# Top-k attention and a hardswish feed-forward on one core: another order of the first loads, warm-up matmuls, and another place for a weight conversion's low words

## The chip, the cores and the metric

The kernel runs on one core of one Trainium2 chip. The metric is the device time of one execution in microseconds, and the kernel before takes 1570.19 us (median of 3 runs, 1567.33 to 1574.13). The engines are called by the profile's names: PE (TensorE, matmuls; PEld its weight loads), DVE (VectorE), ACT (ScalarE), POOL (GpSimd) and SP (SyncE, which here only issues DMAs).

## What is computed

```python
def _attn_ref(q, k, v):                       # each (8, 8, 576, 64)
    scores = scale * np.matmul(q, k.transpose(0, 1, 3, 2))
    kth = np.partition(scores, -32, axis=-1)[..., -32:-31]
    scores = np.where(scores >= kth, scores, -1000000000.0)
    attn = np.exp(scores - np.max(scores, axis=-1, keepdims=True))
    attn = attn / (np.sum(attn, axis=-1, keepdims=True) + 1e-09)
    return np.matmul(attn, v).astype(np.float32)

x = attn_out.transpose(0, 2, 1, 3).reshape(4608, 512)
h = x @ w_in                                  # (512, 2048)
g = h * np.clip(h + 3.0, 0.0, 6.0) / 6.0
out = (g @ w_out).astype(np.float32)          # (2048, 512)
```

Every row of scores keeps its 32 largest values; the attention's output goes through a feed-forward with a hardswish gate. q, k and v come as float32, w_in and w_out as float64, that is as two 32-bit words for each number. The kernel makes float32 of them itself.

## The kernel before

**Tiles.** Two heads make a pair, four pairs make a batch. `Pair.load` (L146) brings k and q of a pair into one tile `landed`: for each of k and q two DMAs of 128 KB and one of 32 KB with the 64 rows that are left beyond 512. `Pair.transpose` (L171) turns them with nine matmuls against `ident` (L177) into a PSUM tile `big`, the only one of its tag (five banks), and ACT copies it to `kq` (kT and qT) and `kr` (the left part of k). A `Duo` is two pairs and one block of 128 queries (or the 64 left ones). `Duo.scores` (L201) forms the score products: a left part for both heads (L232) and 512 columns for each head (L238), then copies them from PSUM to `sc` (L239, L242).

**Top 32.** For each pair of a duo (u = 0, 1) `top` (L249) makes four rounds of MAX8 (L256), two rows each, and, between them, MATCH_REPLACE8 (L260). That is DVE's main work. The rest of the attention follows in slots: `shift` (POOL), `exp` (ACT, L279 and L284), `inverse` (DVE, L293), `weights` (POOL, L303 and a copy to 16-bit halves, L312), `flip` (a DMA transpose, L318), `join` (a copy by ACT or POOL, L324), `values` (PE, L344) and `place` (ACT, L354). The feed-forward (`feed_forward`, L358) is cut into pieces that are put between: h (L371), gate (ACT L379, L381; POOL L385, L386), acc (L391), o (L401). h, acc and pv take PSUM tiles of tag w, of which there are three. The gate's g and, in the conversion, a and y take tiles of tag g, of which there are eight.

**Order.** The order of the instructions on each engine is the program's order (`manual_schedule`). The loop at L572 goes over the duos `m` and eight slots `i` each; in every slot stands a round of `top`, then what the table `usual` or `early` (for the first two duos) has put there, a conversion step, and some pieces of the feed-forward. An engine works its queue in that order and stops at the first instruction that has to wait.

**Conversion of the weights.** There are 32 chunks of 128x512 numbers, 16 of w_in and then 16 of w_out. `convert` (L96) is a generator in stages: a DMA brings the 512 KB of a chunk into `st` (L102); ACT takes the high words' magnitude into `a` (L108), POOL clamps it (L109), and ACT turns the low words into a small fraction `y` (L111); later DVE shifts `a` (L117) and gives `y` the sign (L118); later POOL adds both as integers into the weights (L123). `convert_step` (L495) makes one stage of up to three chunks and asks for another load: chunk n's DVE part stands two steps after its ACT part, its POOL add one step after that. Three steps stand before the loop, and one in each slot.

**The start** (L517 to L529): load pair 0, load two chunks, load pair 1, transpose pair 0, a step, scores of pair 0, a step, load pair 2, a step, transpose pair 1, scores of pair 1, another chunk. Pair 3 is loaded in slot 0. All DMAs are issued by SP. In the before-order of DVE one conversion stands ahead of the first MAX8.

Of the kernel before, what the change touches and what calls it, by code (L numbers as in the profile page):

```python
# [29 lines left out]
def kernel(  # L30
# [32 lines left out]
    gpool = pool("g", 8)  # L63
# [3 lines left out]
    ps_w = pool("ps_w", 3, space=PSUM)  # L67
# [5 lines left out]
    ident = const([P, P], "ident")  # L73
# [4 lines left out]
    w_out = const([P, NFC, DM], "w_out")  # L78
# [9 lines left out]
    def big():  # L88

        return ps_big.tile([P, 5 * 512], F32, tag="big", name="big")  # L90
# [2 lines left out]

    WC = 512

    def convert(dst, src):  # L96

        st = kqpool.tile([P, 2 * WC], U32, tag="kq", name="st")
        nc.sync.dma_start(st[:], src)  # L102
        yield
        words = st[:].rearrange("p (n two) -> p n two", two=2)
        lo, hi = words[:, :, 0], words[:, :, 1]
        a = gpool.tile([P, WC], F32, tag="g", name="a")
        y = gpool.tile([P, WC], F32, tag="g", name="y")
        nc.scalar.activation(a[:], hi.bitcast(F32), AF.Abs)  # L108
        nc.gpsimd.tensor_scalar(a[:], a[:], HI_MOST, HI_LEAST, ALU.min, ALU.max)  # L109

        nc.scalar.activation(y[:], lo, AF.Copy, bias=2.0, scale=2.0**-51)  # L111
        yield

        au, yu = a[:].bitcast(U32), y[:].bitcast(U32)
        nc.vector.tensor_scalar(au, au, 3, None, ALU.logical_shift_left)  # L117
        nc.vector.scalar_tensor_tensor(  # L118
            out=yu, in0=hi, scalar=0x80000000, in1=yu,
            op0=ALU.bitwise_and, op1=ALU.bitwise_or,  # L120
        )
        yield
        nc.gpsimd.tensor_tensor(  # L123
            dst.bitcast(I32), a[:].bitcast(I32), y[:].bitcast(I32), ALU.add
        )

    def weight_chunks():
# [11 lines left out]
    class Pair:  # L139
# [3 lines left out]
            self.b, self.hp = b, hp  # L143
            self.vm, self.vr, self.kr = vms[hp], vrs[hp], krs[b % 2 * NHP + hp]

        def load(self):  # L146
            h0 = 2 * self.hp
            t = self.landed = kqpool.tile([P, 2 * J + 1, 2, D], F32, tag="kq", name="landed")
            for i, src in enumerate((k, q)):
                for hh in range(2):  # L150
                    nc.sync.dma_start(
                        t[:, i * J : (i + 1) * J, hh, :],
                        src[self.b, h0 + hh, 0:JP, :].rearrange("(p j) d -> p j d", j=J),
                    )
                nc.sync.dma_start(
                    t[i * R : (i + 1) * R, 2 * J, :, :],
                    src[self.b, h0 : h0 + 2, JP:S, :].rearrange("h s d -> s h d"),
                )
# [9 lines left out]
                    self.vr[hh * R : (hh + 1) * R, hh, :], v[self.b, h0 + hh, JP:S, :]  # L168
                )

        def transpose(self):  # L171
            kq = kqpool.tile([P, JP + S], F32, tag="kq", name="kq")
            self.kT, self.qT = kq[:, 0:JP], kq[:, JP : JP + S]
            ps = big()
            for j in range(2 * J + 1):
                rows = self.landed[:, j, :, :].rearrange("p h d -> p (h d)")
                nc.tensor.transpose(ps[:, j * P : (j + 1) * P], rows, ident[:])  # L177
            c0 = 2 * JP
            nc.scalar.copy(kq[:, 0:c0], ps[:, 0:c0])
            nc.scalar.copy(kq[:, c0 : c0 + R], ps[:, c0 + R : c0 + 2 * R])  # L180
            for hh in range(2):
                d = slice(hh * D, (hh + 1) * D)
                nc.scalar.copy(self.kr[d, hh, :], ps[d, c0 : c0 + R])

    class Duo:

# [14 lines left out]
        def scores(self, us=(0, 1)):  # L201

            if us[0] == 0:
                self.sc = scpool.tile([P, 2, 2 * (S + R)], F32, tag="sc", name="sc")
                self.den = mpool.tile([P, 2, 2], F32, tag="den", name="den")
            sc, nu = self.sc[:, us[0] : us[-1] + 1, :], len(us)
            ps = big()
            heads = [slice(0, D), slice(D, P)]
            qs = slice(self.qt * P, min(self.qt * P + P, S))
            banks = ps[:, 0 : 4 * 512].rearrange("p (n s) -> p n s", s=512)  # L210
            left = ps[:, 4 * 512 :]
            if self.rest:


                quarters = [
                    (i, hh, d, heads[u ^ hh])
                    for i, u in enumerate(us)
                    for hh, d in enumerate(heads)
                ]
                for i, hh, d, to in quarters:  # L220
                    pr = self.pairs[us[i]]
                    nc.tensor.matmul(banks[to, i, :], pr.qT[d, qs], pr.kT[d, :])
                for i, hh, d, to in quarters:
                    pr = self.pairs[us[i]]
                    nc.tensor.matmul(banks[to, 2 + i, 0:R], pr.qT[d, qs], pr.kr[d, hh, :])
                nc.gpsimd.memset(sc[:, :, S : S + R], 0.0)
                nc.scalar.copy(sc[:, :, 0:JP], banks[:, 0:nu, :])
                nc.scalar.copy(sc[:, :, JP:S], banks[:, 2 : 2 + nu, 0:R])
                return
            for i, u in enumerate(us):  # L230
                pr = self.pairs[u]
                nc.tensor.matmul(  # L232
                    left[:, i * P : (i + 1) * P], pr.qT[:, qs], pr.kr[:].rearrange("p h r -> p (h r)")
                )
            for i, u in enumerate(us):
                pr = self.pairs[u]
                for hh, d in enumerate(heads):
                    nc.tensor.matmul(banks[:, 2 * i + hh, :], pr.qT[d, qs], pr.kT[d, :])  # L238
            nc.scalar.copy(  # L239
                sc.rearrange("p u (h s) -> p (u h) s", h=2)[:, :, 0:JP], banks[:, 0 : 2 * nu, :]  # L240
            )
            nc.scalar.copy(  # L242
                sc[:, :, JP : JP + P], left[:, 0 : nu * P].rearrange("p (u r) -> p u r", r=P)
            )

        def row(self, u, t):
            return self.sc[:, u, t * S : (t + 1) * S]
# [162 lines left out]
    duos = []  # L410
# [77 lines left out]
    def land(count=1):  # L488

        for _ in range(min(count, len(chunks))):  # L490
            c = convert(*chunks.pop(0))
            next(c)
            landing.append(c)

    def convert_step():  # L495


        for c in adding:
            next(c, None)
# [15 lines left out]
        return pairs[b + 1][at - first] if b + 1 < B and 0 <= at - first < NHP else None  # L515

    first = pairs[0]  # L517
    first[0].load()
    land(2)
    first[1].load()  # L520
    first[0].transpose()
    convert_step()
    duos[0].scores((0,))
    convert_step()
    first[2].load()
    convert_step()
    first[1].transpose()
    duos[0].scores((1,))
    land()  # L529

# [41 lines left out]
    for m in range(ND + 3):  # L572
        u = duos[m] if m < ND else None
        for i in range(8):
            if u:
                u.top(i // 4, i % 4)
            if m < 4:
                parts(8 * m + i, False)
            convert_step()
            if m == 0 and i == 0:  # L580
                first[3].load()
            if m == 0 and i in (1, 2):
                first[i + 1].transpose()
            if i == (4 if m == 0 else 1) and m + 1 < ND:
                duos[m + 1].scores()
            if m < 4:
                parts(8 * m + i, True)
            else:
                parts(8 * m + i)
            if m == 0 and i in (1, 4):  # L590
                for p in duos[i // 4].pairs:
                    p.load_values()
            if i == 0:
                p = pair_at(m, 4)
                if p:
# [48 lines left out]
```

## Time and profile before

| what | value |
|---|---|
| span of the profiled execution | 1567.3 us |
| DVE busy | 1466.7 us, 94% |
| PE busy | 1446.8 us, 92% |
| POOL busy | 1143.8 us, 73% |
| ACT busy | 1097.0 us, 70% |
| MAX8 (L256) | 0.74 us each, 1152 of them |
| MATCH_REPLACE8 (L260) | 0.74 us each, 864 of them |
| L117, 32 times | 0.40 / 0.53 / 1.79 us (min / median / max) |
| L118, 32 times | 0.68 / 0.68 / 1.75 us |
| POOL's add L123, 32 times | 1.26 / 1.27 / 1.72 us |
| first MAX8 starts | 13.58 us |
| DVE's last conversion starts | 142.1 us |

The profile is one execution, in microseconds from the span's start. A row of its timeline gives start, length, engine, line, operation and tiles; in square brackets stand the time that the engine sat idle before it and what ended that. An instruction that stands on an engine but waits for a memory port counts as busy there, so a row that is longer than the shortest of its kind can hide a wait. In the chain of work that ended last, "issue" is time for which the profile shows no wait.

### The profile page before, as it was taken

How to read it: one execution, taken by the hardware profiler on the slowest of the kernel's cores; microseconds unless marked ns; L12 is line 12 of the kernel's file. 1: busy time of each engine (PE TensorE's matmuls, PEld its weight loads, DVE VectorE, ACT ScalarE, POOL GpSimd, SP SyncE). 2: the span in 40 equal slices, each digit the busy share in tenths (PEclk: the TensorE clock that was granted, in tenths of full speed). 3: DMA queues.
4: the chain of work that ended last, by engine and by line, in shares of the span. 5: the costliest groups of instructions: out<-in, count | busy, mean ns of one | idle time of the engine just before them, and what ended most of it. 6: DMA issues, size and time to landing. Idle time of an engine off the chain costs nothing.

```text
span 1567.3 us, 28748 instructions
## 1 busy us (share of the span) xinstructions
PE 1446.8 (92%) x10272; PEld 1033.0 (66%) x10272; DVE 1466.7 (94%) x3105; ACT 1097.0 (70%) x1865; POOL 1143.8 (73%) x1264
## 2 busy tenths in 40 slices
PE   5356898899999999999999999999999999999899
PEld 3142665577776777667777777667767777666675
DVE  6999999999999998999999999999999999999910
ACT  6675776777777777777767777777777777777631
POOL 4868688677777788677777779677777778777761
PEclk9977799999999999999999999999999999999999
DMA  8551545444344545345344454344343544433420
GB/s 238 155 188 39 117 87 101 85 92 83 69 83 98 98 83 104 70 100 100 71 85 83 102 99 86 86 99 98 68 83 83 98 99 90 97 68 68 79 43 14
DMA packets 450319, 144.49 MB, mean 92 GB/s; under 512 B 433280, under 2 KB 441472, under 8 KB 450176
## 3 DMA queue, kind: packets, MB, share of 16 engines
q1 hardware_dynamic: 450176, 142.65, 44.2%
q8 instruction: 81, 1.33, 0.3%
q14 instruction: 62, 0.51, 0.1%
HBM read 45.09 MB, written 9.44 MB: 35 GB/s over the span
## 4 chain that ended last, share of the span: by engine, by line
DVE 42%; PE 40%; POOL 6%; ACT 5%; issue 4%; DMA 1%; SPq 1%; POOLq 0%; ACTq 0%
DVE m L256 22%; DVE wk L260 18%; PE h L371 15%; PE acc L391 15%; PE pv L344 5%; PE big L238 3%; POOL e L312 2%; DVE y L118 1%; POOL sc L303 1%; DMA t<-e 1%; ACT eT L324 1%; ACT sc L284 1%; PE big L177 1%; DVE a L117 1%; POOL eT L324 1%
## 5 line engine op out<-in xcount | busy, mean ns | idle before, releaser
L256 DVE MAX8 m<-wk 128x8 f32<-128x576 f32 x864 | 612.6, 745 | 2.2
L391 PE MATMUL acc<-w_out,g 128*128 128x512 f32 x1152 | 522.7, 604 | 17.3 <-POOL g L386 17.3
L371 PEld LDWEIGHTS h<-xT,w_in 128*128 128x128 f32 x4096 | 469.6, 193 | 37.3 <-issue 19.5
L371 PE MATMUL h<-xT,w_in 128*128 128x128 f32 x4096 | 482.7, 277 | 12.0 <-ACT xT L354 12.0
L260 DVE MATCH_REPLACE8 wk<-m,wk 128x576 f32<-128x576 f32 x576 | 423.3, 741 | 0.0
L391 PEld LDWEIGHTS acc<-w_out,g 128*128 128x128 f32 x1152 | 214.4, 193 | 263.5 <-issue 235.8
L303 POOL TENSOR_SCALAR sc<-sc,den 128x576 f32<-128x576 f32 x288 | 213.2, 750 | 206.1 <-DVE den L293 184.6
L312 POOL COPY e<-sc 128x2304 uint16<-128x2304 uint16 (+1 forms) x192 | 320.0, 1677 | 10.1
L324 ACT COPY eT<-t 128x2304 uint16<-128x2304 uint16 (+1 forms) x82 | 216.0, 2635 | 48.1 <-DMA t<-e 47.7
L279 ACT ACTIVATE sc<-sc,m 128x576 f32<-128x576 f32 x288 | 210.6, 779 | 52.3 <-DVE m L256 51.9
L284 ACT ACTIVATE sc<-sc,shift 128x576 f32<-128x576 f32 x288 | 220.4, 770 | 35.3 <-POOL shift L272 33.0
L344 PE MATMUL pv<-eT,vm 128*64 128x128 f32 (+1 forms) x2560 | 163.7, 272 | 56.0 <-ACT eT L324 44.2
L260 DVE MATCH_REPLACE8 wk<-m,sc 128x576 f32<-128x576 f32 x288 | 211.6, 741 | 0.0
L324 POOL COPY eT<-t 128x2304 uint16<-128x2304 uint16 (+1 forms) x78 | 203.5, 2609 | 6.0 <-DMA t<-e 5.8
L344 PEld LDWEIGHTS pv<-eT,vm 128*64 128x64 f32 x2560 | 135.0, 141 | 108.0 <-ACT eT L324 48.9
L256 DVE MAX8 m<-sc 128x8 f32<-128x576 f32 x288 | 203.0, 741 | 1.4 <-ACT sc L242 1.4
L379 ACT ACTIVATE g<-h,three 128x512 f32<-128x512 f32 x144 | 98.9, 687 | 146.7 <-PE h L371 136.0
L386 POOL TENSOR_TENSOR g<-g,hs 128x512 f32<-128x512 f32 x144 | 185.0, 1284 | 12.2 <-POOL g L385 0.2
L239 ACT COPY sc<-big 128x2048 f32<-128x2048 f32 (+1 forms) x65 | 118.9, 1829 | 34.0 <-PE big L238 33.8
L385 POOL TENSOR_SCALAR g<-g 128x512 f32<-128x512 f32 x144 | 88.9, 618 | 68.5 <-ACT g L379 58.9
L238 PE MATMUL big<-kq 64*128 64x512 f32 x512 | 135.5, 649 | 0.0
L381 ACT COPY hs<-h 128x512 f32<-128x512 f32 x144 | 83.8, 582 | 0.0
(47 smaller groups left out, 1030.6 us busy)
## 6 DMA issues: line engine op xcount, KB each, us to landing
landed<-in_k_dram SPq DMA_DIRECT2D x64, 128.0 KB, 2.8
landed<-in_q_dram SPq DMA_DIRECT2D x64, 128.0 KB, 2.9
st<-in_moe_w_in_dram SPq DMA_DIRECT2D x16, 512.0 KB, 5.0
vm<-in_v_dram SPq DMA_DIRECT2D x64, 128.0 KB, 2.3
st<-in_moe_w_out_dram SPq DMA_DIRECT2D x16, 512.0 KB, 6.2
out_dram<-o SPq DMA_DIRECT2D x32, 256.0 KB, 2.5
t<-e SPq DMA_TRANSPOSE x160, 4.6
landed<-in_k_dram SPq DMA_DIRECT2D x32, 32.0 KB, 2.5
```

The source lines that it names most:

```text
L238: nc.tensor.matmul(banks[:, 2 * i + hh, :], pr.qT[d, qs], pr.kT[d, :])
L256: nc.vector.max(self.m[u][:, t, 8 * r : 8 * r + 8], self.cur[t])
L260: nc.vector.match_replace(wk, self.m[u][:, t, 8 * r : 8 * r + 8], self.cur[t], LOWEST)
L279: nc.scalar.activation(row, row, AF.Prelu, bias=m[:, t, TOP_K - 1 : TOP_K], scale=-1.0, alpha=FLAT)
L284: nc.scalar.activation(row, row, AF.Exp, bias=self.less[u][:, t : t + 1], scale=-scale / FLAT, accum_out=self.den[:, u, t : t + 1],)
L303: nc.gpsimd.tensor_scalar(row, row, self.den[:, u, t : t + 1], 1.0, ALU.mult, ALU.mult)
L312: nc.gpsimd.tensor_copy(halves[:, :, to : to + c1 - c0], words)
L324: copy(eT[:, 0 : self.nb, :] .rearrange("p c q -> p (c q)") .bitcast(U16) .rearrange("p (x h) -> p h x", h=2), self.t16[u][:, 0 : 2 * self ...
L344: nc.tensor.matmul(pv[hh * D : (hh + 1) * D, u * w : (u + 1) * w], pr.vm[:, hh, c, :] if c < J else pr.vr[:, hh, :], rhs, start=(c == 0), ...
L371: nc.tensor.matmul(h[:, (f - f0) * P : (f - f0 + 1) * P], w_in[:, i, f * P : (f + 1) * P], xT[:, i, :], start=(i == 0), stop=(i == NHP - 1),)
L386: nc.gpsimd.tensor_tensor(g[:], g[:], hs[:], ALU.mult)
L391: nc.tensor.matmul(acc[:], gs[f // nf][:, f % nf * P : (f % nf + 1) * P], w_out[:, f, :], start=(f == 0), stop=(f == NFC - 1),)
```

## The change

There are four edits. The first batch is loaded first: q of pair 0 is issued by ACT instead of SP, the three other pairs are loaded ahead of most weight chunks, and the loads of chunks follow one by one; one conversion step before the loop is gone. For pair 0 the transposes go to three PSUM tiles of tag w, each copied as soon as it is ready, and the part of q that the first scores do not need is copied later; of the first scores the left part is copied first and then each head by itself. A warmed-up TensorE: DVE clears one block of w_out, and PE multiplies it twice into a PSUM tile that nothing reads, while the first loads are under way. The low words y no longer take a tile of tag g: for the first 16 chunks (those of w_in) ACT writes them to a PSUM tile of tag w and DVE writes the signed word to the weights' place; for the 16 chunks of w_out ACT writes them to the weights' place at once. POOL's add then reads a and the destination.

```diff
-    def convert(dst, src):
+    def convert(dst, src, early):
...
-        y = gpool.tile([P, WC], F32, tag="g", name="y")
+        y = ps_w.tile([P, WC], F32, tag="w", name="y")[:] if early else dst
...
-        nc.scalar.activation(y[:], lo, AF.Copy, bias=2.0, scale=2.0**-51)
+        nc.scalar.activation(y, lo, AF.Copy, bias=2.0, scale=2.0**-51)
...
-            out=yu, in0=hi, scalar=0x80000000, in1=yu,
+            out=dst.bitcast(U32), in0=hi, scalar=0x80000000, in1=y.bitcast(U32),
...
-            dst.bitcast(I32), a[:].bitcast(I32), y[:].bitcast(I32), ALU.add
+            dst.bitcast(I32), a[:].bitcast(I32), dst.bitcast(I32), ALU.add
...
-        def load(self):
+        def load(self, queue=None):
...
-            for i, src in enumerate((k, q)):
+            for i, (src, eng) in enumerate(((k, nc.sync), (q, queue or nc.sync))):
                 for hh in range(2):
-                    nc.sync.dma_start(
+                    eng.dma_start(
...
+            if first:
+                ps = [ps_w.tile([P, 512], F32, tag="w", name="kqp") for _ in range(3)]
+                turn(ps[0], range(J))
+                turn(ps[1], [J, 2 * J])
+                turn(ps[2], range(J + 1, 2 * J))
+                nc.scalar.copy(self.kT, ps[0][:])
+                nc.scalar.copy(kq[:, JP : JP + P], ps[1][:, 0:P])
+                copy_left(ps[1][:, P:])
+                self.later = [
+                    (kq[:, JP + P : c0], ps[2][:, 0 : JP - P]),
+                    (kq[:, c0 : c0 + R], ps[1][:, P + R : 2 * P]),
+                ]
+                return
...
+            if us == (0,):
+                (to, src), rest = copies
+                copies = [rest, (to[:, 0, :], src[:, 0, :]), (to[:, 1, :], src[:, 1, :])]
+            for copy in copies:
+                nc.scalar.copy(*copy)
...
-            c = convert(*chunks.pop(0))
+            c = convert(*chunks.pop(0), early=len(chunks) >= NFC)
...
-    first[0].load()
-    land(2)
+    nc.vector.memset(w_out[:, 0, :], 0.0)
+    ps = big()
+    for _ in range(2):
+        nc.tensor.matmul(ps[:, 0:DM], w_out[:, 0, 0:P], w_out[:, 0, :])
+    first[0].load(nc.scalar)
     first[1].load()
-    first[0].transpose()
+    land()
+    first[2].load()
+    land()
+    first[0].transpose(first=True)
+    duos[0].scores((0,))
+    for copy in first[0].later:
+        nc.scalar.copy(*copy)
     convert_step()
-    duos[0].scores((0,))
+    first[3].load()
+    first[1].transpose()
     convert_step()
-    first[2].load()
-    convert_step()
-    first[1].transpose()
     duos[0].scores((1,))
     land()
...
-            if m == 0 and i == 0:
-                first[3].load()
```

More of the change, by code (lines that the diff above doesn't have):

```diff
@@ L106, in convert @@
         a = gpool.tile([P, WC], F32, tag="g", name="a")
-        y = gpool.tile([P, WC], F32, tag="g", name="y")
+        y = ps_w.tile([P, WC], F32, tag="w", name="y")[:] if early else dst
         nc.scalar.activation(a[:], hi.bitcast(F32), AF.Abs)
         nc.gpsimd.tensor_scalar(a[:], a[:], HI_MOST, HI_LEAST, ALU.min, ALU.max)
-        nc.scalar.activation(y[:], lo, AF.Copy, bias=2.0, scale=2.0**-51)
+        nc.scalar.activation(y, lo, AF.Copy, bias=2.0, scale=2.0**-51)
         yield
-        au, yu = a[:].bitcast(U32), y[:].bitcast(U32)
+        au = a[:].bitcast(U32)
         nc.vector.tensor_scalar(au, au, 3, None, ALU.logical_shift_left)
         nc.vector.scalar_tensor_tensor(
-            out=yu, in0=hi, scalar=0x80000000, in1=yu,
+            out=dst.bitcast(U32), in0=hi, scalar=0x80000000, in1=y.bitcast(U32),
             op0=ALU.bitwise_and, op1=ALU.bitwise_or,
@@ L154, in load @@
                     )
-                nc.sync.dma_start(
+                eng.dma_start(
                     t[i * R : (i + 1) * R, 2 * J, :, :],
@@ L169, in load_values, with transpose, turn, copy_left @@
                 )
-        def transpose(self):
+        def transpose(self, first=False):
             kq = kqpool.tile([P, JP + S], F32, tag="kq", name="kq")
             self.kT, self.qT = kq[:, 0:JP], kq[:, JP : JP + S]
+            c0 = 2 * JP
+            def turn(ps, tiles):
+                for i, j in enumerate(tiles):
+                    rows = self.landed[:, j, :, :].rearrange("p h d -> p (h d)")
+                    nc.tensor.transpose(ps[:, i * P : (i + 1) * P], rows, ident[:])
+            def copy_left(ps):
+                for hh in range(2):
+                    d = slice(hh * D, (hh + 1) * D)
+                    nc.scalar.copy(self.kr[d, hh, :], ps[d, 0:R])
+            if first:
[11 more added lines that the diff above has]
+                return
             ps = big()
[L175 to L178, printed above, removed]
+            turn(ps, range(2 * J + 1))
             nc.scalar.copy(kq[:, 0:c0], ps[:, 0:c0])
             nc.scalar.copy(kq[:, c0 : c0 + R], ps[:, c0 + R : c0 + 2 * R])
-            for hh in range(2):
-                d = slice(hh * D, (hh + 1) * D)
-                nc.scalar.copy(self.kr[d, hh, :], ps[d, c0 : c0 + R])
+            copy_left(ps[:, c0:])
     class Duo:
@@ L238, in scores @@
                     nc.tensor.matmul(banks[:, 2 * i + hh, :], pr.qT[d, qs], pr.kT[d, :])
[L239 to L244, printed above, removed]
+            copies = [
+                (sc.rearrange("p u (h s) -> p (u h) s", h=2)[:, :, 0:JP], banks[:, 0 : 2 * nu, :]),
+                (sc[:, :, JP : JP + P], left[:, 0 : nu * P].rearrange("p (u r) -> p u r", r=P)),
+            ]
+            if us == (0,):
[3 more added lines that the diff above has]
+                nc.scalar.copy(*copy)
         def row(self, u, t):
```

## The prediction

> **What bounds the kernel now.** I read the page's busy times first, then the chain, then who VectorE (DVE) waited for.
>
> ```profile
> PE 1446.8 (92%) x10272; PEld 1033.0 (66%) x10272; DVE 1466.7 (94%) x3105; ACT 1097.0 (70%) x1865; POOL 1143.8 (73%) x1264
> ...
> DVE 42%; PE 40%; POOL 6%; ACT 5%; issue 4%; DMA 1%; SPq 1%; POOLq 0%; ACTq 0%
> ```
>
> DVE and TensorE (PE) are both nearly full and share the chain. In order of time the chain lies on DMA issues and DVE until about 172 us, on PE from 177 to 590, on DVE from 604 to about 1480, and on PE to the end (DVE's last work ends near 1502, PE has 65 us left). The waits of DVE, all that there are:
>
> ```profile
> DVE den L293 <- ACT den L289: 13.9, 5, 5.9
> DVE a L117 <- POOL a L109: 13.6, 2, 10.3
> DVE m L256 <- ACT sc L242: 1.4, 1, 1.4
> ```
>
> After 144 us DVE idles some 13 us in all, so a shift of DVE's early work should reach the end. PE's full stretch also hangs on DVE: it starts at 176.87, after POOL's eT copy at 174.05, behind a MAX8 that ends at 173.5. Its 65 us tail is work in a fixed order. So I count only what DVE gains before 172 us, and carry that over one for one.
>
> Three things there cost DVE time. First, the start (the timeline: start, length, instruction, idle before it and releaser):
>
> ```profile
> 4.54 1.09 PE L177 MATMUL big<-ident,landed 128*128 128x128 f32 x4 [4.54 <-DMA landed<-in_k_dram]
> 6.66 1.30 PE L177 MATMUL big<-ident,landed 128*128 128x128 f32 x5 [1.03 <-DMA landed<-in_q_dram]
> 9.54 0.77 PE L232 MATMUL big<-kr,kq 128*128 128x128 f32 x2 [1.58 <-ACT kr L183]
> 10.24 2.08 PE L238 MATMUL big<-kq 64*128 64x512 f32 x4
> 12.37 1.01 ACT L239 COPY sc<-big 128x1024 f32<-128x1024 f32 x1 [1.42 <-PE big L238]
> 13.58 1.42 DVE L256 MAX8 m<-sc 128x8 f32<-128x576 f32 x2 [1.43 <-ACT sc L242]
> ```
>
> The first MAX8 waits for k, then q, nine transposes, copies, a score product and its copies: 13.58 us. One weight conversion (L117, L118) fits into that wait. Second, conversions that stand behind POOL:
>
> ```profile
> 54.91 2.10 POOL L312 COPY e<-sc 128x2304 uint16<-128x2304 uint16 x1
> ...
> 55.51 1.78 DVE L117 TENSOR_SCALAR a<-a 128x512 uint32<-128x512 uint32 x1
> 56.98 1.43 POOL L123 TENSOR_TENSOR w_in<-a,y 128x512 int32<-128x512 int32 x1
> ...
> 57.22 1.75 DVE L118 SCALAR_TENSOR_TENSOR y<-st,y 128x512 uint32<-128x512 uint32 x1
> ```
>
> L117 takes 0.41 us undisturbed and L118 0.68; here they end 0.28 after L312 and 0.56 after L123. They count as busy, but they wait. Third, a shortage of buffers of tag g:
>
> ```profile
> 134.70 0.69 ACT L379 ACTIVATE g<-h,three 128x512 f32<-128x512 f32 x1 [9.07 <-POOL w_out L123]
> ...
> 137.23 1.48 DVE L117 TENSOR_SCALAR a<-a 128x512 uint32<-128x512 uint32 x1 [3.30 <-POOL a L109]
> ```
>
> ScalarE (ACT) holds its queue 9.07 us until an add of POOL frees a g buffer; the next a is late by that, and DVE idles 3.30 us.
>
> **What the Trainium skill says.** (1) "SBUF — State Buffer", "Who interferes with whom": a DVE instruction with two SBUF inputs contends with a GpSimd instruction that reads SBUF; with at most one SBUF input, outside the two-port modes, it does not; the loser blocks fully. The rows above agree. (2) "VectorE: DVE Perf Modes", errata section: a fixed 58 cycles from SBUF, 120 from PSUM, at 0.96 GHz; the difference is an estimate of 0.065 us. No row before shows L118 from PSUM. (3) "TensorE: Matmul & The Clock Gate", Part 1: PE runs at half clock until a free-running window of about 3.4 us has been busy. The trace agrees by durations: L238 takes 2.08 us for 4 records here and 1.99 for 8 at 185.25. (4) "DMA: Bandwidth & Descriptors", "Issuing engines are not separate DMA queues": a second issuing engine saves issue time only.
>
> **The change, part by part.**
>
> *Start.* q's three DMAs move to ACT's queue and no longer wait behind k's (0.72 to 2.77). Before, k landed at 4.5 and q at 6.6, each about 1.8 after its last issue. Both together are 576 KB, 2.3 us at the 249 GB/s that the stage from 10 to 20 us moves, so q lands between 4.6 and 5.8; I take 5.2. The warm-up: a DVE memset of 128x512 (no row; 0.41 to 0.68 by L117 and L118), then two matmuls of 128x512, four records of 0.81 us (133.03, 8 records in 6.5 us, half clock): PE is held from 1.4 to 4.7, no later than k. Transposes at half clock: four to 5.8, two to 6.3, three more to 7.0. ACT: 512 columns of k 0.58 (as L381), 128 of q 0.27, kr twice 0.22, to 7.1, while the last three transposes run. L232 then takes 0.7, L238 2.08: 10.0. The score copies wait for both, but the order is now left part 0.27, first head 0.58, and MAX8 of row 0 needs only these: 10.7. If the clock is released at once, up to 0.7 of transposes, 0.4 and 1.0 of the products go too: near 8.8. The window's phase decides; I take 9.9, a gain of 3.7 (2.8 to 4.8).
>
> *Chunks later.* The first batch takes the queue, so chunk 0 is issued after nine DMAs near 7 and lands (median 5.0) near 12; +0.66 ACT +0.61 POOL is 13.2, where DVE wants it at 9.9+2.96=12.9. Chunk 1 comes after six more loads, near 12, lands near 17, ready 18.2, wanted near 17.1. Behind the waiting L117 stand all MAX8s. Loss 1.2 (0 to 3). One conversion less lies before the first MAX8, so one more lies between: 0.33+0.60, say 1.0.
>
> *Low words by PSUM.* The first 16 chunks' L118 has one SBUF input and doesn't wait for POOL. In the trace 3 of these 16 are longer by 1.07 and 3 by 0.41: 4.4 us. POOL is earlier, so L117 can still hit an add. Working the round at 51 to 62 through by hand (L109 0.54 earlier, L312 ends 56.5, L117 56.8, L118 57.4, second L117 behind L123 to 60.1, L118 60.7 instead of 61.96) gives 1.26; three rounds and chunk 3's 0.41 give 4.2. Minus up to 16 x 0.065 = 1.0 for PSUM, take 3.6 (1.5 to 4.4). ACT's y waits for the L118 three chunks earlier (three PSUM buffers of tag w); behind it stand exp and score copies, but ACT keeps over a conversion's lead, so I cost it at nothing.
>
> *Straight to the destination.* No conversion takes two g buffers. Of the 9.07 us wait DVE gets its 3.30 us back, at most, as POOL itself is busy there; smaller ACT waits of the same kind (9.1 on w_in, 6.8 and 4.4 on w_out) go too, and reach DVE little. Take 3.2 (0 to 5). L118 of w_out still has two SBUF inputs: nothing.
>
> Sum: 3.7 - 1.2 - 1.0 + 3.6 + 3.2 = 8.3, so 1570.2 - 8.3, rounded, 1562.
>
> **Rivals.** *Gains partly absorbed, near 1567:* chunk waits of 3, PSUM only 1.5, buffers only 1.5: 2.8-3-1+1.5+1.5 = 1.8 to 3. For it: POOL from 108 to 137 is busy most of the time and L117 stays in its way; PE is full from 177, and its half clock at 172 to 180 comes and goes with the window. Against: DVE has no other slack. *Slower, near 1579:* chunks 1 and 2 behind the batch cost 5 us each if the queue's slow issues (0.94, 1.55 us before) spread, PSUM buffers shared with pv and h hold ACT and PE for 3, the extra conversion 1, PE starts its full stretch at half clock (3): 17, against 8 gained. For it: DMA is at a share of 1.06 from 10 to 20 us. Against: chunks have 5 us between uses.
>
> **How the numbers follow.** As forecast 0.5; absorbed 0.42; slower 0.08. The forecast sits close to the 0.5% bound (1562.3), so its chance is that of gaining more than 7.9 us. All low ends give a loss of about 0.5 (2.8-3-1+1.5+0), which with the case of partial slowing and 2 us of scatter reaches 1571; all high ends give 4.8-0-1+4.4+5 = 13, with scatter 1555.
>
> **What would show it.** Right: first MAX8 between 9 and 11; no w_in L118 over 0.8; ACT's 9 us wait gone; DVE's last MAX8 some 8 us earlier, PE's tail unchanged. Wrong: L117 waiting over 3 us on chunks, L117 longer by what L118 lost, DVE waits after 144 grown, or L118 from PSUM above 0.9.

## The result and the profile after

| | before | after |
|---|---|---|
| median time | 1570.61 us (6 runs, 1567.33 to 1574.13) | 1565.14 us (6 runs, 1563.29 to 1566.63) |
| span of the profiled execution | 1567.3 us | 1562.2 us |

The ratio is 0.9965, with a 95% interval of 0.995 to 0.9979: 5.5 us faster, where 8.3 were forecast. The time lies in the range. The forecast case was "faster by more than 7.9 us"; what came lies between it and the rival "absorbed, near 1567".

The page of the kernel after, busy times and the chain that ended last:

```profile
PE 1443.5 (92%) x10276; PEld 1030.4 (66%) x10276; DVE 1467.0 (94%) x3106; ACT 1096.0 (70%) x1868; POOL 1137.8 (73%) x1264
...
PE 50%; DVE 32%; POOL 6%; ACT 4%; issue 4%; DMA 1%; SPq 1%; POOLq 0%; ACTq 0%
```

VectorE's busy time is the same within 0.3 us, although the kernel is faster: shares say nothing here, and the early stages have to be read one by one. What VectorE waited for, over the whole span of the kernel after (total, times, longest):

```profile
DVE den L320 <- ACT den L316: 14.1, 4, 5.9
DVE m L283 <- ACT sc L271: 8.8, 1, 8.8
DVE a L118 <- POOL a L110: 1.1, 2, 0.8
```

(Line numbers moved: the shift of `a` is L118 now, the sign L119, the inverse L320, MAX8 L283, the clamp L110, the add L124.) The 13.6 us on POOL's clamp are 1.1. Before, 10.3 of them lay ahead of the first MAX8, which only waited 1.4 on its own; now that MAX8 waits 8.8 by itself. Only 3.30 of the 13.6 was time to win later on. The start, in the timeline of the kernel after:

```profile
1.47 3.78 PE L550 MATMUL big<-w_out 128*128 128x512 f32 x4 [1.47 <-DVE w_out L547]
5.81 1.42 PE L182 MATMUL kqp<-ident,landed 128*128 128x128 f32 x9 [0.56 <-DMA landed<-in_k_dram]
7.89 0.46 PE L256 MATMUL big<-kr,kq 128*128 128x128 f32 x2 [0.66 <-issue]
8.28 1.13 PE L262 MATMUL big<-kq 64*128 64x512 f32 x4
9.46 1.24 ACT L271 COPY sc<-big 128x128 f32<-128x128 f32 x3 [1.67 <-PE big L262]
10.24 1.42 DVE L283 MAX8 m<-sc 128x8 f32<-128x576 f32 x2 [8.83 <-ACT sc L271]
13.87 0.43 DVE L118 TENSOR_SCALAR a<-a 128x512 uint32<-128x512 uint32 x1 [0.76 <-POOL a L110]
17.97 0.43 DVE L118 TENSOR_SCALAR a<-a 128x512 uint32<-128x512 uint32 x1 [0.30 <-POOL a L110]
32.22 0.17 DVE L320 RECIPROCAL den<-den 128x2 f32<-128x2 f32 x1 [2.34 <-ACT den L316]
```

The first MAX8 starts 3.34 us earlier (13.58 before). Two short waits for chunks follow, as forecast. The last line was not forecast: by the first inverse, which started at 33.03 before, only 0.81 us of the 3.34 is left.

What the sign instruction takes (view of its line; minimum, median, maximum in ns, then first and last start):

```profile
L119 DVE SCALAR_TENSOR_TENSOR w_in<-st,y x16: 673/676/681, 14.2 to 73.2; 128x512 uint32<-128x512 uint32 x16
L119 DVE SCALAR_TENSOR_TENSOR w_out<-st,w_out x16: 676/1091/2579, 76.9 to 140.8; 128x512 uint32<-128x512 uint32 x16
```

For w_in, where y comes from PSUM, none is longer than 0.681 us. For w_out, where both inputs are in SBUF, the longest was 1.75 before and is 2.58 now. The timeline of the kernel after shows that one, on both engines:

```profile
134.50 1.47 POOL L330 TENSOR_SCALAR sc<-sc,den 128x576 f32<-128x576 f32 x2
135.47 0.78 DVE L118 TENSOR_SCALAR a<-a 128x512 uint32<-128x512 uint32 x1
136.03 2.17 POOL L339 COPY e<-sc 128x2304 uint16<-128x2304 uint16 x1
136.17 2.58 DVE L119 SCALAR_TENSOR_TENSOR w_out<-st,w_out 128x512 uint32<-128x512 uint32 x1
...
140.00 0.85 DVE L118 TENSOR_SCALAR a<-a 128x512 uint32<-128x512 uint32 x1
```

L118 ends with POOL's L330 plus 0.28, L119 with POOL's L339 plus 0.55.

**A ledger.** Apart from the conversions, VectorE makes the same instructions in the same order in both kernels, so the start times of the 160 inverses in two profiles can be subtracted (an inverse is the reciprocal of a row's sum, L320). The lead of the kernel after over the one before, in us:

| inverse (start before) | 33.0 | 49.0 | 65.6 | 82.2 | 120.0 | 139.2 | 149.9 | 573 | 945 | 988 | 1501.7 | span |
|---|---|---|---|---|---|---|---|---|---|---|---|---|
| lead | 0.81 | 2.07 | 3.41 | 4.74 | 5.07 | 6.61 | 2.95 | 2.9 | 3.1 | 4.6 | 4.53 | 5.1 |

The start leaves 0.81, three rounds with w_in's conversions 1.26, 1.34 and 1.33, and the stretch with w_out's conversions gains 1.9 and then loses 3.66 between the sixth and the seventh inverse. From there to 590 us the lead is constant to 0.1 us: what VectorE gains early is carried one for one. At 590 to 602 and once near 958 something else adds about 1.6 (experiment 9).

### The profile page after: what moved, and what is told of

It is laid out like the page before. It is cut to its first block, busy times and chain, and to the rows that moved or that the text cites. A ratio compares the mean times of both kernels' runs of the same rounds, so it can differ in the third digit from the quotient of the medians.

```text
span 1562.2 us, 28737 instructions
## 1 busy us (share of the span) xinstructions
PE 1443.5 (92%) x10276; PEld 1030.4 (66%) x10276; DVE 1467.0 (94%) x3106; ACT 1096.0 (70%) x1868; POOL 1137.8 (73%) x1264
## 3 DMA queue, kind: packets, MB, share of 16 engines
q8 instruction: 81, 1.33, 0.3%
## 4 chain that ended last, share of the span: by engine, by line
PE 50%; DVE 32%; POOL 6%; ACT 4%; issue 4%; DMA 1%; SPq 1%; POOLq 0%; ACTq 0%
PE h L398 20%; PE acc L418 19%; DVE m L283 16%; DVE wk L287 13%; PE pv L371 6%; PE big L262 5%; POOL e L339 2%; POOL sc L330 1%; POOL eT L351 1%; DMA t<-e 1%; PE big L182 1%; PE big L256 1%; DVE w_out L119 1%; DVE a L118 1%; POOL g L413 1%
## 5 line engine op out<-in xcount | busy, mean ns | idle before, releaser
L283 DVE MAX8 m<-wk 128x8 f32<-128x576 f32 x864 | 613.2, 746 | 2.2
L398 PE MATMUL h<-xT,w_in 128*128 128x128 f32 x4096 | 483.6, 278 | 14.0 <-ACT xT L381 11.7
L330 POOL TENSOR_SCALAR sc<-sc,den 128x576 f32<-128x576 f32 x288 | 212.8, 748 | 205.7 <-DVE den L320 174.0
L339 POOL COPY e<-sc 128x2304 uint16<-128x2304 uint16 (+1 forms) x192 | 320.1, 1677 | 10.1
L283 DVE MAX8 m<-sc 128x8 f32<-128x576 f32 x288 | 203.3, 743 | 8.8 <-ACT sc L271 8.8
L271 ACT COPY sc<-big 128x256 f32<-128x256 f32 (+3 forms) x131 | 136.6, 1095 | 31.4 <-PE big L262 31.2
```

The source lines that it names most:

```text
L283: nc.vector.max(self.m[u][:, t, 8 * r : 8 * r + 8], self.cur[t])
L330: nc.gpsimd.tensor_scalar(row, row, self.den[:, u, t : t + 1], 1.0, ALU.mult, ALU.mult)
L339: nc.gpsimd.tensor_copy(halves[:, :, to : to + c1 - c0], words)
L398: nc.tensor.matmul(h[:, (f - f0) * P : (f - f0 + 1) * P], w_in[:, i, f * P : (f + 1) * P], xT[:, i, :], start=(i == 0), stop=(i == NHP - 1),)
```

## The experiments

My theory after the result: the gain is the memory port in w_in's rounds alone; the start is used up at the first inverse; and y written straight to w_out's place earns nothing or costs. The rival was the recorded sum, each part worth about what the forecast gives it. Each run is compared with the kernel before on its own chip.

**1. The kernel after again** (no edit), for the scatter.

> The changed kernel once more, to see what of its ledger repeats. In its first profile VectorE was 6.6 us ahead of the kernel before at 132.6 us, 2.95 us ahead from 147 us on, and 1.5 us more came at 958 us where one wait on the inverse is missing. Theory A (the early ledger is fixed by the order of the instructions, the gain at 958 us is scatter of a DMA): again 2.9 +-0.3 at 147 us, and the 1.5 at 958 us need not come back. Theory B (both follow from the change): both come back within 0.3. Time 1565 +-2 in either case.

1564.88 us, ratio 0.9971 (0.9958 to 0.9984). Lead 0.91 at the first inverse, 3.05 at the seventh, 3.95 late. So the early ledger repeats to 0.1 us, the late one to about 0.6. The 1.5 at 958 us came back too: it is a wait in the profile of before, with which both are compared (experiment 9).

**2. The low words of w_out in tag g again.**

```diff
-        y = ps_w.tile([P, WC], F32, tag="w", name="y")[:] if early else dst
+        y = ps_w.tile(...)[:] if early else gpool.tile([P, WC], F32, tag="g", name="y")[:]
```

> The changed kernel, but the low words of the 16 chunks of w_out go to tiles of tag g again; those of w_in stay in PSUM. Theory A (the port): straight to the destination is worth about nothing, since the sign instruction of w_out still has two SBUF inputs and waits for POOL instead of idling on a late clamp: 1564 to 1566, VectorE's lead at 147 us between 2.0 and 4.0. Theory B (my forecast): it is worth 3.2 us and the loss between 133 and 147 us has another cause: about 1568, lead at 147 us near 0, and the 9 us wait of ScalarE for a g tile is back.

1562.44 us, ratio 0.9952 (0.9939 to 0.9964): 2.4 us faster than the change. The lead at the seventh inverse is 6.10, against 3.05. So here "straight to the destination" does not win 3.2, it loses about 3; that is less than both theories gave it (nothing, or a gain of 3.2). ScalarE waits for g tiles again (L112 on POOL's add, 7.4 us in three pieces between 112 and 150 us), and VectorE does not wait for it: it is busy through that whole stretch, as it is in the change. The first eleven of w_out's conversions (shift and sign) take 18.8 us in both kernels, the last five 9.7 here and 12.4 in the change.

**3. The low words of all 32 chunks by PSUM.**

```diff
-            c = convert(*chunks.pop(0), early=len(chunks) >= NFC)
+            c = convert(*chunks.pop(0), early=True)
```

> The changed kernel, but the low words of all 32 chunks go by PSUM. Theory A (the port): no sign instruction of w_out waits for POOL (all 0.68 us), VectorE is 3 to 5 us further ahead at 147 us than with the change (6 to 8 instead of 2.95), time 1560 to 1562. Rival (PSUM tiles): y, pv, h and acc share three tiles, ScalarE and TensorE hold each other up there; VectorE then waits on late clamps, lead at 147 us under 2, time 1567 to 1575.

1556.2 us, ratio 0.9914 (0.9901 to 0.9928): 8.7 us faster than the change in experiment 1, the best of all. The view of the sign's line:

```profile
L119 DVE SCALAR_TENSOR_TENSOR w_in<-st,y x16: 672/675/684, 13.7 to 72.8; 128x512 uint32<-128x512 uint32 x16
L119 DVE SCALAR_TENSOR_TENSOR w_out<-st,y x16: 669/674/678, 76.5 to 131.8; 128x512 uint32<-128x512 uint32 x16
```

All 32 are undisturbed: 21.6 us together, against 28.2 in the change. The lead at the seventh inverse is 11.92, 9.0 more than in the change: the signs give 6.6 of it, and w_out's shifts, which are held up less, 2.0 (11.9 us against 13.8). Theory A had 6 to 8 for the lead and 1560 to 1562 for the time, so it was too small; of the rival's hold-up by PSUM tiles nothing reaches VectorE. The destination is still written straight, so it is not the place of the result that cost, but the second SBUF input.

**4. No low words by PSUM, all straight to the destination.**

```diff
-            c = convert(*chunks.pop(0), early=len(chunks) >= NFC)
+            c = convert(*chunks.pop(0), early=False)
```

> The changed kernel, but no low words go by PSUM: ScalarE writes y to the weights' place for w_in too, so its sign instruction has two SBUF inputs there as well. Theory A (the port): the sign instructions of w_in wait for POOL again (some of 1.07 and 0.41 us more), VectorE loses 1.3 us in each of three rounds, 3.9 us in all: about 1569, lead at 77 us 0.8 to 1.2 instead of 4.7. Rival (the gain on w_in comes from freed g tiles, not from the port): within 1 us of the change.

1568.68 us, ratio 0.9995 (0.9987 to 1.0004): no gain. In the three w_in rounds the lead stands still (1.02 at the second to fourth inverse), and w_in's sign takes up to 1.75 us. As theory A has it, PSUM alone makes the difference of 3.8 us to the change on the same chip; in the ledger it is 3.76.

**5. No warm-up.**

```diff
-    nc.vector.memset(w_out[:, 0, :], 0.0)
-    ps = big()
-    for _ in range(2):
-        nc.tensor.matmul(ps[:, 0:DM], w_out[:, 0, 0:P], w_out[:, 0, :])
```

> The changed kernel without the memset and the two warm-up matmuls. Theory A (what the start gains is swallowed by the later waits for chunk 0, chunk 1 and the first inverse, 0.76, 0.30 and 2.34 us in the changed kernel's profile): transposes back at 2.2 us for nine, score products near 2.8, first MAX8 near 11.7 instead of 10.24, but these three waits shrink and the lead at 32 us (first inverse) stays within 0.5 of 0.8; time within 1 us of the change (1564 to 1566). Rival (as my forecast had it, the start goes through one for one): lead 1.4 lower all the way, about 1566.5.

1565.3 us, ratio 0.9971 (0.9961 to 0.9982), the same as the change. TensorE's start in this kernel:

```profile
5.86 2.15 PE L182 MATMUL kqp<-ident,landed 128*128 128x128 f32 x9 [5.86 <-DMA landed<-in_k_dram]
8.19 0.76 PE L256 MATMUL big<-kr,kq 128*128 128x128 f32 x2 [0.18 <-ACT kr L187]
8.89 2.08 PE L262 MATMUL big<-kq 64*128 64x512 f32 x4
```

The transposes take 2.15 us instead of 1.42 and the products 2.08 instead of 1.13; the first MAX8 comes at 11.80, 1.56 later. But the first inverse is only 0.74 later. VectorE waits 0.5 less for chunks (0.6 instead of 1.1); the wait for the exp does not shrink, against theory A (2.33 instead of 2.34). Its lead of 0.07 is a little lower than A allowed, too. As far as the chain shows, the 0.74 do not come from the first scores at all: chunk 3 lands 0.75 later (23.43 instead of 22.68), and the exp stands behind it (see the part on the start below). At the seventh inverse this kernel is still 0.75 behind, and in the medians 0.2 to 0.4, which these intervals can't tell from nothing.

**6. q of the first pair on SyncE again.**

```diff
-    first[0].load(nc.scalar)
+    first[0].load()
```

> The changed kernel, but q of pair 0 is issued by SP behind k. Theory A (swallowed): k lands near 4.5 instead of 5.8 and q near 6.7, first MAX8 at most 0.8 us later, lead at 32 us as before within 0.4 (though the later loads and chunks are issued 2 us later, which could cost up to 1), time 1564 to 1566. Rival (the second queue is worth its issue time): first MAX8 2 us later, time 1567.

1568.47 us, ratio 0.9992 (0.9985 to 0.9998). Its 22 executions go from 1565.2 to 1571.1, and the profiled one was the fastest (span 1563.4), so the profile explains only part: there the transposes of k start at 4.75 instead of 5.81 and those of q at 6.45, all nine are over at 7.25 (7.23 in the change), the first MAX8 starts at 10.00 (10.24 in the change), but VectorE waits longer for the first two chunks (2.5 us instead of 1.1), and the lead is -0.50 instead of 0.81 at the first inverse, 1.66 instead of 2.95 at the seventh. Chunk 3, issued behind three DMAs more, lands at 24.00 instead of 22.68, as much later as the first inverse. So the second queue wins nothing at the first MAX8, and 1.3 through the chunks behind it. Theory A is right on the first MAX8, but wrong on the lead and on the time, and the rival is wrong on the first MAX8. Where the slower executions lose the rest was not profiled.

**7. The conversions of the change with the start of the kernel before.** `convert` and `land` as after, the start of the program, the first transposes and the order of copies as before.

> The start of the kernel before (order of loads, transposes in one PSUM tile, no warm-up, one conversion ahead of the first MAX8) with the conversions of the change. Theory A (the change's gain comes from the port on w_in; the start is worth little): lead 3 to 4.5 at 82 us, time 1565 to 1567, i.e. 3 to 5 faster than the kernel before. Rival (start worth 3, conversions worth 2.5): 1567.5 to 1568.5.

1563.97 us, ratio 0.9965 (0.9953 to 0.9977), no slower than the change, and a little faster than theory A said. The lead is 3.75 at 82 us, as A has it, and 3.72 at the seventh inverse. Between the sixth and seventh inverse it loses 1.9, where the change loses 3.66: it has one conversion there, with a sign of 2.58 us, and the change has two.

**8. The start of the change with the conversions of the kernel before.** `y` in tag g for all chunks, in the sign and in the add as before.

> The start of the change with the conversions of the kernel before (y of all chunks in tag g). Theory A: lead 1 us at 32 us and no growth to 82 us, one conversion more behind it, so about 0 at 147 us: 1568.5 to 1570.5. Rival (start worth 3 by itself): 1566 to 1567.5.

1574.6 us, ratio 1.0033 (1.002 to 1.0046): slower than before, by some 5 us, and slower than both theories said. The lead is 0.47 at the first inverse, 0.42 at the sixth and then -4.12. VectorE's timeline shows what stands there:

```profile
136.81 1.49 DVE L118 TENSOR_SCALAR a<-a 128x512 uint32<-128x512 uint32 x1 [3.30 <-POOL a L110]
...
146.45 1.48 DVE L118 TENSOR_SCALAR a<-a 128x512 uint32<-128x512 uint32 x1 [2.45 <-POOL a L110]
```

The first of these is in the kernel before too. The second is the last chunk, behind the sixth inverse. Counting conversions on VectorE between inverses explains it: before, six stand ahead of the first inverse and one behind the sixth; with the new start, five and two. The step that was taken out of the start has to be made at the end of the conversions, and there it is a bad one: 2.45 of waiting and 0.60 and 1.40 to the starts that follow, 4.45 of the 4.54 lost.

**9. The kernel before again** (no edit), since the first profile of it waits 1.43 us for ScalarE's exp at 958 us and none of the later ones does.

> The kernel before, unchanged, in a second profile. In the first, VectorE waited 1.43 us for ScalarE's exp at 958.00, and none of the kernels since shows that wait, not even the one that runs behind (direct destination, no PSUM), so about 1.5 us of each difference of spans hangs on it. Theory A, scatter of one execution: the wait is under 0.3 us here, the span is near 1566 and the change's real gain on the chip's middle run stays at 5.5 only if other executions lose the same elsewhere. Theory B, a part of the old order: the wait stands again at 1.2 to 1.6 us near 958 and the span is 1567 to 1568.

1570.91 us in one execution, span 1569.1. The early part repeats to 0.3 us. Of the five inverses that waited after 170 us in this profile, these three differ from the first one; the other two (2.18 and 5.92 us, near the end) stand in every kernel:

```profile
602.08 0.16 DVE L293 RECIPROCAL den<-den 128x1 f32<-128x1 f32 x1 [4.93 <-ACT den L289]
980.61 0.17 DVE L293 RECIPROCAL den<-den 128x1 f32<-128x1 f32 x1 [0.71 <-ACT den L289]
1315.09 0.16 DVE L293 RECIPROCAL den<-den 128x1 f32<-128x1 f32 x1 [1.54 <-ACT den L289]
```

The wait of 958 is gone, so theory B falls. But the span is not shorter, against A: the wait at 602 is 1.1 longer and another stands at 1315. After 170 us the waits on the exp sum to 13.3 and 15.3 us in the two profiles of before, to 11.7 and 12.4 in the two of after, and to between 11.5 and 16.1 in the other kernels. They come where the order of the work changes (590 to 602, 958 to 980, 1302 to 1320 us), and not in all executions in the same places. Of the 5.1 us between the two spans 1.6 lie there. Whether the change causes them, two profiles of each can't tell.

**10. All low words by PSUM, with the start of before** (the edits of 3 and 7 together).

> The low words of all 32 chunks by PSUM and straight to the destination, with the start of the kernel before (no warm-up, two chunks ahead of the second pair, q on SyncE, three conversions before the loop). Theory A (the start is worth nothing at the end, since what it wins at the first MAX8 goes to a later exp and to one conversion more behind the sixth inverse): within 1.5 of the kernel with all by PSUM and the new start, so 1555 to 1558, and the loss between the sixth and the seventh inverse, 1.2 there, is near zero. Theory B (the start is worth its 3.7, only hidden behind w_out's sign instructions so far, which here no longer wait for POOL): 1559 to 1561.

1556.71 us, ratio 0.9918 (0.9905 to 0.9932). As theory A has it: the same as experiment 3 within the intervals; the lead at the seventh inverse is 11.74 against 11.92, and 0.27 is lost behind the sixth, against 1.2. The first MAX8 starts at 13.18, 3.3 later than in experiment 3. All of the start's edits together are worth nothing that shows at the end, where the intervals would hide some 2 us, and 0.2 at the seventh inverse.

**11. All by PSUM, chunk 1 loaded ahead of the third pair.**

```diff
-    land()
+    land(2)
     first[2].load()
-    land()
```

> All low words by PSUM, new start, and weight chunk 1 ahead of the third pair's six loads in SyncE's queue. Theory A (VectorE's two chunk waits, 0.6 and 0.6 us in the kernel with all by PSUM, are a matter of the queue): the second wait goes, the first stays, the first inverse is 0.3 to 0.6 earlier unless the exp wait of 2.3 takes it back: 1555 to 1556.5. Theory B (that exp wait ends last, and it hangs on loads that this edit makes later): nothing at the first inverse or a loss up to 1, 1556 to 1558.

1557.22 us, ratio 0.992 (0.9906 to 0.9934), no gain, as theory B has it (the edit is against experiment 3). One of the two waits for chunks went (0.3 is left in all), as A has it, but the first inverse is not earlier. In this run the warm-up did not release the clock in time:

```profile
5.90 2.15 PE L182 MATMUL kqp<-ident,landed 128*128 128x128 f32 x9 [0.65 <-DMA landed<-in_k_dram]
...
11.44 1.42 DVE L283 MAX8 m<-sc 128x8 f32<-128x576 f32 x2 [10.02 <-ACT sc L271]
```

Behind a warm-up of the same 3.78 us, ended at 5.25, the nine transposes took 2.15 us, as without any. In six profiles with one unbroken row of nine transposes behind the same warm-up they took 1.17 to 1.25, in the change's 1.42. The first MAX8 is 1.57 later than in experiment 3, the first inverse 0.58. The 0.58 is again what chunk 3 lands later (22.88 against 22.30), and the wait for the exp is 2.34 as there. Whether the edit makes chunk 3 later can't be told from one profile, since it lands between 22.29 and 23.43 in the other profiles with the change's loads.

**12. All by PSUM, a third conversion step ahead of the loop.**

```diff
     duos[0].scores((1,))
+    convert_step()
     land()
```

> All low words by PSUM, new start, and a third conversion step after the scores of row 1, as many as the kernel before has ahead of its loop. Theory A (the new start only moved one conversion from ahead of the first inverse to behind the sixth): six conversions before the first inverse and one, not two, behind the sixth; the lead at the first inverse falls from 1.2 by 1 to 3, since chunk 2 has to be waited for, and the stretch behind the sixth inverse gives 1.3 back: 1555 to 1557.5. Theory B (the conversion can be taken in the exp wait of 2.3 for nothing): the lead at the first inverse stays at 1.2 and 1.3 is won at the end: 1554.5 to 1555.2.

1558.46 us, ratio 0.9932 (0.9917 to 0.9946): about 2 slower than experiment 3 (against which the edit is) and 1 above theory A's range. The first MAX8 in VectorE's timeline:

```profile
15.22 1.42 DVE L283 MAX8 m<-sc 128x8 f32<-128x576 f32 x2
```

No wait stands in its brackets, since the conversion ahead of it has taken it: VectorE waits 12.9 us for chunk 0 with the scores of row 0 ready near 10. The lead at the first inverse is -1.26, 2.46 less than in experiment 3 (A gave 1 to 3 less), and behind the sixth inverse 0.95 comes back. For the lead A holds and B does not. With this order of loads the step is dear in either place.

## Why the prediction was right or wrong

The recorded experiments fit in one table: the lead over the first profile of before at the seventh inverse (149.88 us there), and the median.

| low words of w_in / of w_out | start of before | start of the change |
|---|---|---|
| g / g | 0 (0.23 in 9); 1570.6 | -4.12; 1574.6 |
| destination / destination | | -0.81; 1568.7 |
| PSUM / g | | 6.10; 1562.4 |
| PSUM / destination | 3.72; 1564.0 | 2.95 and 3.05; 1565.1 and 1564.9 |
| PSUM / PSUM | 11.74; 1556.7 | 11.92; 1556.2 |

*What bounds it: right.* VectorE's early lead goes through to the end: 2.95 at the seventh inverse, 2.9 at 573 us, and over the table 16 us of lead make 18.4 us of median. Its account of the chain is too simple: in the kernel before the chain lies mostly on POOL and ScalarE from 110 to 139 us, and on PE, not on DVE, from 1027 to about 1265. The lead came through the second of these all the same (4.6 at 988 us, 4.5 at 1501.7).

*Low words by PSUM: right.* Forecast 3.6 (hand-worked round 1.26, three of them); measured 1.26, 1.34 and 1.33 a round and 3.76 in all (change against experiment 4). The estimated price of reading PSUM, up to 1.0, is not there: 0.676 us at the median from PSUM, 0.677 at the least from SBUF in the kernel before. "SBUF — State Buffer", "Who interferes with whom", of the Trainium skill says that an instruction of VectorE with at most one SBUF input does not contend with GpSimd, outside the two-port modes; experiment 3 agrees for the sign, 32 of 32 between 0.669 and 0.684. The shift has one SBUF input too and still waits there (up to 1.48 us in place of 0.41), which that condition on the modes leaves room for.

*Start: the step is right, its place in the sum is not.* First MAX8 at 10.24, forecast 9.9; gain 3.34, forecast 3.7. The parts went otherwise than worked out: k landed at 5.8, not 4.5, since q was fetched at the same time; the clock was released for the transposes (1.42 us for nine, 2.15 without a warm-up); and the copies waited for both products, as forecast. What failed is that the sum then only subtracts waits for chunks (1.2 forecast, 1.06 measured) and carries the rest over. A wait of 2.34 us for the exp of ScalarE was not in it (0.55 before). First two rows of the kernel before, then four of the change (the first of these is a piece of its chain):

```profile
28.33 1.01 ACT L179 COPY kq<-big 128x1024 f32<-128x1024 f32 x1 [0.99 <-PE big L177]
33.03 0.17 DVE L293 RECIPROCAL den<-den 128x2 f32<-128x2 f32 x1 [0.55 <-ACT den L289]
...
18.06 4.62 DMA st<-in_moe_w_in_dram
22.70 0.66 ACT L109 ACTIVATE a<-st 128x512 f32<-128x512 f32 x1 [2.48 <-DMA st<-in_moe_w_in_dram]
27.53 1.01 ACT L205 COPY kq<-big 128x1024 f32<-128x1024 f32 x1 [1.04 <-PE big L182]
29.00 1.44 ACT L306 ACTIVATE sc<-sc,m 128x576 f32<-128x576 f32 x2
```

In the change ScalarE waits 2.48 us for chunk 3 until 22.70, then copies pair 3 at 27.53, then makes the exp at 29.00: the chain that ends last at the first inverse runs over loads, not over the first scores. The trace of before has the same: the load of pair 3, its copy at 28.33, then the exp, so the first scores were not what ended last there either. The other profiles leave little doubt. In the nine that have the start of the change, whole or with one part undone (experiment 12, which has a step more, left out), the first inverse starts 9.51 to 9.53 us after ScalarE begins on chunk 3 (L109), whether the first MAX8 starts at 9.87 or at 11.80. Experiment 10 shows the worth of the start with the rest equal: nothing beyond the intervals.

*One more conversion: right that there is one, wrong place.* The forecast put it between the MAX8s of the first round, at 1.0. There are five between the first MAX8 and the first inverse in both kernels; the sixth moved behind the sixth inverse. In the change that stretch holds two conversions of 4.89 us of VectorE in place of one of 1.09 and loses 3.66; with an undisturbed sign (experiment 3) it loses 1.2, close to the forecast. The other 2.5 are collisions with POOL, which belong to the next term.

*Straight to the destination: the step that failed.* "Take 3.2 (0 to 5)" and "L118 of w_out still has two SBUF inputs: nothing". ScalarE's wait of 9.07 us and VectorE's of 3.30 did go. But w_out's 16 signs grew from 14.7 to 17.4 us and its shifts from 13.1 to 13.8. The rows at 134 to 140 show what one shift and one sign waited for. One could think that POOL, busy for 33.0 of the 38 us from 112 to 150 against 28.1 before, is simply there more often. The other runs speak against that alone: it is busy for 33.4 in experiment 2, where the cost is not there, and for 35.9 in experiment 3. What differs between experiment 2 and the change is which instructions of POOL stand beside the last five conversions (9.7 us there, 12.4 here); why they come to stand so is not shown. The table adds what the forecast could not see: the two remedies overlap. Without PSUM the destination is worth 3.3 (-4.12 to -0.81), about as forecast, though there it takes away two waits, of 3.30 and 2.45, and 0.5 of it is only an earlier chunk 3 (the lead at the first inverse is 1.00 against 0.47); with w_in by PSUM the 3.30 wait is gone already and the destination costs 3.05. Why the shortage of g tiles doesn't reach VectorE in experiment 2 is not settled; ScalarE's waits there are up to 2.8 us each in place of one of 9.07.

*The sum.* By the ledger 0.81 + 3.93 + 0.33 + 1.54 - 3.66 = 2.95, where 8.3 was forecast for the same place. The median fell by 5.5: the spans differ by 5.1, as 1.6 more lie in the later waits of experiment 9 and 0.6 in the tail (65.6 before, 65.0 after), neither of which the forecast claimed. Part of the agreement is therefore luck: the range held the time, but a third of the forecast's gain was missing, and of its three gains two, the start and the destination, were not there. (Its sum of all low ends is off: 2.8 - 3 - 1 + 1.5 + 0 is a gain of 0.3, not a loss of 0.5.) Of the rival "absorbed" the small worth of the buffers came, not the long waits for chunks; of the rival "slower" nothing came in the change (VectorE's two waits for chunks are 1.06, not 10), though experiment 8 shows that its start with the old conversions is slower, for another reason.

*The signs to look for.* First MAX8 between 9 and 11: yes. No sign of w_in over 0.8: yes. The 9 us wait gone: yes. The last of VectorE's work 8 us earlier: no, 4.5. PE's tail unchanged: nearly (65.6 to 65.0). Of the signs against, none came: the longest wait for a chunk is 0.76, no sign from PSUM is over 0.68, VectorE's waits after 144 us went from 13.3 to 11.7, and of the 4.5 us that w_in's signs lost (15.3 to 10.8) its shifts took back only 0.6 (12.0 to 12.6).

## What to carry to other kernels

When two edits each remove the same wait, price the second with the first already in place, and ask what the engine that no longer waits will collide with: here the buffers were freed, and the last conversions then came to stand beside other work of POOL, which cost more than the buffers had. An operand moved from SBUF to PSUM cured the collision where it was done, and doing it for the other half of the weights too was worth more than the whole change. A faster start counts only as far as the next instruction that waits for another chain, so follow the chain to the first point where the engines meet before pricing it: here loads ended last at the first inverse, before and after. And a step that is taken out of the start is still to be paid for where it lands.

## What the runs showed of the hardware

- VectorE's sign, a 128x512 scalar_tensor_tensor, took 0.67 to 0.68 us whether its second input lay in PSUM or, undisturbed, in SBUF. ScalarE's y was somewhat faster into PSUM: 0.604/0.622/0.657 us (minimum, median, maximum in the change) against 0.647/0.662/0.713 into SBUF.
- Two queues delayed the first load: k's transposes started at 4.52 to 4.75 us in five profiles with q behind it, at 5.68 to 6.01 in nine with q beside it, and the nine transposes were over at 7.25 in experiment 6, at 6.86 to 7.23 in the seven profiles with q beside it and a warm-up that worked. "DMA: Bandwidth & Descriptors", "Issuing engines are not separate DMA queues", of the skill says that a second engine saves the issue alone. The trace agrees: with q's three DMAs off its queue SyncE issued chunk 3 at 18.06 instead of 19.20, and the chunk landed 1.3 us earlier. For 17 us from 0.72 on SyncE did nothing but issue 24 DMAs, one behind the other.
- The same warm-up of two matmuls (3.4 to 3.8 us) does not release TensorE's clock in every execution: nine transposes behind it took 1.17 to 1.42 us in seven profiles and 2.15 in an eighth. "TensorE: Matmul & The Clock Gate", Part 1, of the skill describes a free-running window of activity that decides on the clock; that is in keeping with it. The profile's own column of the granted clock shows 1.00 in these microseconds in all of them, also where the transposes took 2.15, so durations have to be read.
